# A top-k attention and gated MLP kernel with its slot pipeline made one slot shorter and TensorE's work put in a new order

## The chip, the cores and the metric

The kernel runs on one core of a Trainium2 chip. The core has five engines with instruction streams of their own: TensorE (PE, with its weight loads shown as PEld), VectorE (DVE), ScalarE (ACT), GpSimd (POOL) and SyncE (SP), which issues the transfers. Each works through its stream in the order in which the program was written; they wait for each other by semaphores. The metric is the device time of one execution in microseconds; lower is better.

## The reference, cut to what matters

Attention for 8 batches, 8 heads, 576 queries and keys, 64 numbers per head, in which each query keeps its 32 largest scores only; then a feed-forward block on the heads side by side (4608 tokens of 512 numbers, 2048 hidden), all in float32:

```python
scores = scale * np.matmul(q, k.transpose(0, 1, 3, 2))
kth = np.partition(scores, -top_k, axis=-1)[..., -top_k:-top_k + 1]
scores = np.where(scores >= kth, scores, -1000000000.0)
scores = scores - np.max(scores, axis=-1, keepdims=True)
attn = np.exp(scores)
attn = attn / (np.sum(attn, axis=-1, keepdims=True) + 1e-09)
attn_out = np.matmul(attn, v)
x = attn_out.transpose(0, 2, 1, 3).reshape(B * S, H * D)
h = x @ w_in
g = h * (1.0 / (1.0 + np.exp(-1.702 * h)))
return g @ w_out
```

The two weights come in float64, 16 MB in all, and are rounded to float32 on the chip.

## The kernel before, in words

**Slots.** Work on attention is cut into slots. A slot is 128 queries of a pair of heads, so its scores are a tile `sc` of 128 rows and twice 576 columns. A batch has four full query tiles by four pairs of heads, 16 slots, and the last 64 queries of two pairs put together make two more: 18 slots a batch, N = 144 in all. `slots` lists them in order; before, each batch has its full tiles first and its last queries at the end.

**Stages of a slot.** `scores` (L217) multiplies q by k on TensorE, two heads at once on the two halves of the array's rows, and ScalarE copies the result out (L224). `topk` is a chain of 14 VectorE operations on the two heads: eight times the next eight largest (MAX8, L233), and in between removal of those found (MATCH_REPLACE8, L236). `bounds` makes two small columns on GpSimd (L252, L253); `exponentials` on ScalarE raises what lies below the cut out of the way (L261) and takes the exponential with its sum (L263). `divide` takes the reciprocal of the sums on VectorE (L271, L273) and multiplies both halves of `pr` by it on GpSimd (L276). `turn_main` transposes eight blocks of `pr` on TensorE and `turn_ends` a ninth (L285), with copies on ScalarE (L286). `values` multiplies by v (L308), using half of the array's columns for each head, and ScalarE copies the result into `xT` (L320).

**The feed-forward block.** When all four pairs of a query tile are in `xT`, the tile is `ready`. From then on each slot does one group of four of its sixteen blocks: `hidden` (L349, into one PSUM tile `ph`), `tanh` on ScalarE (L366), `gate` on VectorE (L373, (tanh + 1) times ph, into `gT`), and `project` (L387, added up in `po` over four groups), after which `ob` is copied out (L392) and stored. The last queries of two batches fill one tile of 128 rows together. There are 36 tiles and so 144 groups, as many as there are slots.

**The order in a slot.** Everything is written out by hand, slot by slot, in `slot(n)`; no scheduler changes it. On TensorE it stands as: turn_main of slot n-2, hidden, turn_ends of n-2, prepare (transposes of q and k for coming slots, L187 and L193), scores of n+1, values of n-2, project. On ScalarE: exponentials of n-1, copies of the turn, of prepare, tanh, copies of the scores, of the values, then the rounding of weights for slot n+1. On VectorE: topk of n with the two small operations of `divide` for n-1 after the sixth of its 14, then gate.

**Weights.** The 32 pieces of 128 x 512 are loaded as raw words and rounded in the first slots (`round_piece`): three ScalarE operations (L131 to L133), a shift on VectorE (L137) and two operations on GpSimd (L138, L139). Five pieces belong to slot 0, three to each of the next nine. `pieces` alternates groups of `w_in` and `w_out`.

**Buffers that matter.** `ps_t`, two PSUM buffers, is shared by transposes and values; `ph` has one; `raws` has six; `qkt`, the transposed q and k, five of each.

The functions that the diff touches, with the line numbers of the profile:

Of the kernel before, what the change touches and what calls it, by code (L numbers as in the profile page):

```python
# [8 lines left out]
AF = mybir.ActivationFunctionType  # L9
ALU = mybir.AluOpType  # L10
ENG = mybir.EngineType
F32 = mybir.dt.float32
U32 = mybir.dt.uint32
# [3 lines left out]
P = 128  # L17
# [11 lines left out]
def kernel(  # L29
# [41 lines left out]
    FIRST = (TAIL, 0)  # L71
    MAIN = (0, FULL + 2 * TAIL)
    SCALE = 1.0 / float(D) ** 0.5
    assert D == 64 and 2 * TAIL == P and C == NP * P and C == PIECE and B % 2 == 0
    assert TOPK == 32 and NP == 4 and NF == 4 and NG == 4 and CC == 4

    const = ctx.enter_context(tc.tile_pool(name="const", bufs=1))
    pool = lambda name, bufs, **kw: ctx.enter_context(tc.tile_pool(name=name, bufs=bufs, **kw))
    raws = pool("raws", 6)
    loads = pool("loads", 2)  # L80
    vals = pool("vals", 6)
    qkt = pool("qkt", 5)
    scp = pool("scp", 3)
    prp = pool("prp", 2)
    lefts = pool("lefts", 1)
    small = pool("small", 4)
    ptp = pool("ptp", 2)
    xtp = pool("xtp", 3)
    xtt = pool("xtt", 1)
    gtp = pool("gtp", 3)  # L90
    thp = pool("thp", 2)
    osp = pool("osp", 2)
    ps_s = pool("ps_s", 2, space=PSUM)
    ps_t = pool("ps_t", 2, space=PSUM)
    ps_h = pool("ps_h", 1, space=PSUM)
# [5 lines left out]
    wout = const.tile([P, FC, C], F32, name="wout")  # L101


    pieces = []
    for g in range(NG + 1):
        pieces += [(c, g) for c in range(CC) if g < NG] + [(None, f) for f in range((g - 1) * G, g * G) if g]
    raw = {}

    def load_piece(n):
# [8 lines left out]
    def round_piece(n):  # L118

        c, g = pieces[n]
        dst = wout[:, g, :] if c is None else win[:, c, g * PIECE : (g + 1) * PIECE]
        words = raw.pop(n)[:].rearrange("p (n w) -> p n w", w=2)
        low, high = words[:, :, 0], words[:, :, 1].bitcast(F32)  # L130
        nc.scalar.activation(dst, high, AF.Abs, scale=REBASE)  # L131
        nc.scalar.activation(high, high, AF.Sign)  # L132
        nc.scalar.mul(out=low.bitcast(I32), in_=low, mul=2.0**-29)  # L133

        def shift():
            bits, whole = dst.bitcast(U32), dst.bitcast(I32)
            nc.vector.tensor_scalar(bits, bits, 3, None, op0=ALU.logical_shift_left)  # L137
            nc.gpsimd.tensor_tensor(out=whole, in0=whole, in1=low.bitcast(I32), op=ALU.add)  # L138
            nc.gpsimd.tensor_tensor(out=dst, in0=dst, in1=high, op=ALU.mult)  # L139

        return shift


    qT, kT, vv = {}, {}, {}
# [53 lines left out]

    slots = []
    for b in range(B):  # L200
        slots += [(b, t, (hp, hp)) for t in range(NF) for hp in range(NP)]
        slots += [(b, NF, (hp, hp + 1)) for hp in range(0, NP, 2)]
    N = len(slots)
    PER = N // B
    st = [{} for _ in slots]
# [20 lines left out]
    def topk(n):  # L226

        sc = st[n]["sc"]
        top = st[n]["top"] = small.tile([P, 2, TOPK], F32, name="top")
        left = lefts.tile([P, 2, S], F32, name="left")  # L230

        def largest(r, i):
            nc.vector.max(top[:, i, 8 * r : 8 * r + 8], (left if r else sc)[:, i, :])  # L233

        def remove(r, i):
            nc.vector.match_replace(  # L236
                left[:, i, :], top[:, i, 8 * r : 8 * r + 8], (left if r else sc)[:, i, :], LOWEST
            )

        ops = []  # L240
        for r in range(TOPK // 8):
            ops += [lambda r=r, i=i: largest(r, i) for i in range(2)]
            if r < TOPK // 8 - 1:
                ops += [lambda r=r, i=i: remove(r, i) for i in range(2)]
        return ops
# [22 lines left out]
    def divide(n):  # L268
        den, pr = st[n]["den"], st[n]["pr"]
        some = small.tile([P, 2], F32, name="some")  # L270
        nc.vector.tensor_scalar_add(some[:], den[:], 1e-9)  # L271
        rden = small.tile([P, 2], F32, name="rden")
        nc.vector.reciprocal(rden[:], some[:])  # L273
        for i in range(2):
            on = pr[:, i * S : (i + 1) * S]
            nc.gpsimd.tensor_scalar(on, on, rden[:, i : i + 1], None, op0=ALU.mult)  # L276

    def turn(n, first, cols, blocks):
        pr = st[n]["pr"]
# [8 lines left out]
    def turn_main(n):  # L288
        for i in range(2):
            turn(n, i * NF, MAIN[i], NF)  # L290

    def turn_ends(n):

        turn(n, 2 * NF, FULL, 1)
# [39 lines left out]

    ready = []
    hidden_at = {"g": 0}
    to_gate, to_project = [], []
    proj = {}

    def hidden():  # L340
        if not ready:
            return
        xT, rows = ready[0]
        g = hidden_at["g"]
        ph = ps_h.tile([P, G, P], F32, name="ph")
        for i in range(G):
            f = g * G + i
            for c in range(CC):
                nc.tensor.matmul(  # L349
                    ph[:, i, :],  # L350
                    lhsT=win[:, c, f * P : (f + 1) * P],
                    rhs=xT[:, c, :],
                    start=(c == 0),
                    stop=(c == CC - 1),
                )
        to_gate.append((ph, g, rows))
        hidden_at["g"] = (g + 1) % NG
        if g == NG - 1:
            ready.pop(0)

    def tanh():

        if to_gate and len(to_gate[-1]) == 3:
            ph, g, rows = to_gate.pop()
            th = thp.tile([P, G, P], F32, name="th")
            nc.scalar.activation(th[:], ph[:], AF.Tanh, scale=0.851 / RAISE)  # L366
            to_gate.append((ph, g, rows, th))

    def gate():
        if to_gate:  # L370
            ph, g, rows, th = to_gate.pop()
            gT = gtp.tile([P, G, P], F32, name="gT")
            nc.vector.scalar_tensor_tensor(  # L373
                out=gT[:], in0=th[:], scalar=1.0, in1=ph[:], op0=ALU.add, op1=ALU.mult
            )
            to_project.append((gT, g, rows))

    def project():
        if not to_project:
            return  # L380
        gT, g, rows = to_project.pop(0)
        if g == 0:
            proj["po"] = ps_p.tile([P, C], F32, name="po")
        po = proj["po"]
        for i in range(G):
            f = g * G + i
            nc.tensor.matmul(  # L387
                po[:], lhsT=gT[:, i, :], rhs=wout[:, f, :], start=(f == 0), stop=(f == FC - 1)
            )
        if g == NG - 1:  # L390
            ob = osp.tile([P, C], F32, name="ob")
            nc.scalar.mul(out=ob[:], in_=po[:], mul=0.5 / RAISE**2)  # L392
            for on, row in rows:
                nc.sync.dma_start(out[row : row + on.stop - on.start, :], ob[on, :])
# [4 lines left out]
    def at(n, fn, *args):  # L399
        later.setdefault(n, []).append((fn, args))  # L400

    READY = ((-6, -5), (-2, -1), (-1, 0), (0, 1))
    FETCH = ((-12, -11), (-9, -8), (-5, -4), (-1, 0))
    VALUES = (-8, -7, 1, 2)
    by_slot = {}
    for x in range(NPIECE):
        by_slot.setdefault(max(x - 2, 0) // 3, []).append(x)
    for hp in range(NP):  # L410
        for name in "qk":
            at(max(hp - 2, -1), load, name, 0, hp)
# [6 lines left out]
    for b in range(1, B):  # L419
        for hp in range(NP):  # L420
            for i, name in enumerate("qk"):
                at(b * PER + FETCH[hp][i], load, name, b, hp)
                at(b * PER + READY[hp][i], prepare, name, b, hp)
            at(b * PER + VALUES[hp], load_v, b, hp)
    rounding = {}

    def begin_rounding(n):
        rounding[n] = [round_piece(x) for x in by_slot.get(n, [])]

    def slot(n):  # L430
        todo = later.pop(n, [])
        for fn, args in todo:
            if fn is not prepare:
                fn(*args)
        if 0 <= n - 1 < N:
            bounds(n - 1)
            exponentials(n - 1)
        if 0 <= n - 2 < N:
            turn_main(n - 2)
        hidden()  # L440
        if 0 <= n - 2 < N:
            turn_ends(n - 2)
        for fn, args in todo:
            if fn is prepare:
                fn(*args)
        tanh()
        if n + 1 < N:
            scores(n + 1)
        if 0 <= n - 2 < N:
            values(n - 2)  # L450
        project()
        begin_rounding(n + 1)
        chain = topk(n) if 0 <= n < N else []
        more = rounding.pop(n, [])
        for i, op in enumerate(chain):
            op()
            if i == 5 and 0 <= n - 1 < N:
                divide(n - 1)
            if i and more:
                more.pop(0)()  # L460
        if n == N:
            divide(n - 1)
        gate()

    with tc.manual_schedule():
        for n in range(-1, N + 2):
            slot(n)
        n = N + 2
        while ready or to_project:
            slot(n)  # L470
            n += 1

# [29 lines left out]
```

## Time and profile before

| | |
|---|---|
| time, median of 3 runs | 1684.97 us (1683.83 to 1685.44) |
| span of the profiled run | 1684.1 us |
| TensorE busy | 1596.2 us, 95% |
| VectorE busy | 1539.8 us, 91% |
| ScalarE busy | 1007.0 us, 60% |
| GpSimd busy | 633.7 us, 38% |

A page gives for each engine the time in which it was doing an instruction. Matmuls are pipelined: a new one starts before the last one's end, and their ends are modelled, so for TensorE it is the distance between starts that tells how fast it works. Groups of instructions are named by line, engine, operation and tiles, with their count, busy time, mean length and what ended the idle time before them. VectorE's two groups of the chain, MAX8 and MATCH_REPLACE8, take about 750 ns for each operation; the product on GpSimd (L276) takes 1723 ns, the gate (L373) 677 ns, the copy of a turn (L286) about 470 ns.

### The profile page before, as it was taken

To read this page: it belongs to the slowest core of one execution; us is meant where nothing else is said; L and a number is where in the kernel's file an instruction comes from. 1 tells how busy PE (TensorE), PEld (TensorE's weight loads), DVE (VectorE), ACT (ScalarE), POOL (GpSimd) and SP (SyncE) were. 2 spreads that over 40 slices of the span, in tenths; PEclk is the share of its full clock that TensorE was granted. 3 is DMA by queue.
4 is the path that set the end of the run, shared out by engine and by line. 5 is a ranking of instruction groups with operands and counts; after the bars stand their busy time and mean duration, and the time that the engine had idled before them with its cause. 6 is when DMAs were issued, how large, how long until landed. Compare 5 with 4: busy or idle time off the path is not lost.

```text
span 1684.1 us, 31437 instructions
## 1 busy us (share of the span) xinstructions
PE 1596.2 (95%) x11824; PEld 1176.2 (70%) x11824; DVE 1539.8 (91%) x3344; ACT 1007.0 (60%) x2181; POOL 633.7 (38%) x652
## 2 busy tenths in 40 slices
PE   3459999899999999999999999999999999999998
PEld 2346777677777777777777777777777777777776
DVE  5899999999999999999999999999999999899940
ACT  6787566555655666555655566556665566555530
POOL 5887333333333332333333333333323333333320
PEclk6579999899999999999999999999999999999999
DMA  8341100100101101010000101011010100000000
GB/s 241 119 127 34 28 22 21 42 17 20 36 21 29 29 17 29 13 34 22 21 22 21 36 21 36 15 35 27 16 29 21 35 22 21 22 7 7 7 8 13
DMA packets 125719, 56.55 MB, mean 34 GB/s; under 512 B 116864, under 2 KB 116864, under 8 KB 125568
## 3 DMA queue, kind: packets, MB, share of 16 engines
q1 hardware_dynamic: 125568, 54.55, 12.2%
q8 instruction: 93, 1.52, 0.4%
q14 instruction: 58, 0.48, 0.1%
HBM read 45.09 MB, written 9.44 MB: 32 GB/s over the span
## 4 chain that ended last, share of the span: by engine, by line
PE 90%; ACT 5%; DVE 2%; issue 1%; SPq 1%; POOL 0%; DMA 0%; POOLq 0%; DVEq 0%; ACTq 0%
PE po L387 30%; PE ph L349 30%; PE o L308 11%; PE s_ps L217 10%; PE tp L285 8%; PE tp L187 2%; ACT raw L132 1%; DVE top L233 1%; DVE left L236 1%; ACT raw L133 1%; ACT pr L263 1%; ACT win L131 1%; ACT k_t L189 1%; ACT wout L131 0%; ACT sc L261 0%
## 5 line engine op out<-in xcount | busy, mean ns | idle before, releaser
L276 POOL TENSOR_SCALAR pr<-pr,rden 128x576 f32<-128x576 f32 x288 | 492.9, 1723 | 682.6 <-DVE rden L273 424.7
L233 DVE MAX8 top<-left 128x8 f32<-128x576 f32 x864 | 611.8, 752 | 0.0
L387 PE MATMUL po<-wout,gT 128*128 128x512 f32 x1152 | 532.0, 605 | 0.0
L349 PE MATMUL ph<-xT,win 128*128 128x128 f32 x4096 | 480.0, 276 | 1.9 <-DVE gT L373 1.9
L349 PEld LDWEIGHTS ph<-xT,win 128*128 128x128 f32 x4096 | 469.2, 192 | 3.1 <-DVE gT L373 2.1
L236 DVE MATCH_REPLACE8 left<-top,left 128x576 f32<-128x576 f32 x576 | 423.9, 745 | 0.0
L387 PEld LDWEIGHTS po<-wout,gT 128*128 128x128 f32 x1152 | 207.1, 189 | 229.0 <-issue 227.7
L261 ACT ACTIVATE sc<-sc,cut 128x576 f32<-128x576 f32 x288 | 207.2, 767 | 193.6 <-POOL cut L252 193.6
L286 ACT COPY pt<-tp 128x512 f32<-128x512 f32 (+1 forms) x432 | 188.6, 470 | 219.2 <-PE tp L285 218.8
L285 PEld LDWEIGHTS tp<-ident,pr 128*128 128x128 f32 x1296 | 156.3, 142 | 126.3 <-issue 62.3
L285 PE MATMUL tp<-ident,pr 128*128 128x128 f32 x1296 | 193.3, 276 | 48.2 <-ACT pt L286 44.8
L263 ACT ACTIVATE pr<-sc,low 128x576 f32<-128x576 f32 x288 | 218.9, 761 | 0.0
L233 DVE MAX8 top<-sc 128x8 f32<-128x576 f32 x288 | 204.5, 755 | 12.2 <-ACT sc L224 11.3
L236 DVE MATCH_REPLACE8 left<-top,sc 128x576 f32<-128x576 f32 x288 | 212.9, 751 | 0.0
L224 ACT COPY sc<-s_ps 128x576 f32<-128x576 f32 x288 | 170.4, 645 | 57.3 <-PE s_ps L217 55.2
L217 PE MATMUL s_ps<-k_t,q_t 64*128 64x288 f32 (+1 forms) x1280 | 189.5, 444 | 0.9 <-ACT k_t L189 0.9
L308 PEld LDWEIGHTS o<-pt,v_l 128*64 128x64 f32 x2560 | 131.8, 140 | 58.2 <-ACT th L366 35.5
L308 PE MATMUL o<-pt,v_l 128*64 128x128 f32 (+1 forms) x2560 | 166.0, 274 | 0.0
L373 DVE SCALAR_TENSOR_TENSOR gT<-th,ph 128x512 f32<-128x512 f32 x144 | 97.5, 677 | 54.1 <-ACT th L366 53.8
L252 POOL TENSOR_SCALAR cut<-top 128x2 f32<-128x2 f32 x144 | 31.9, 222 | 273.9 <-DVE top L233 272.8
L217 PEld LDWEIGHTS s_ps<-k_t,q_t 64*128 64x128 f32 (+1 forms) x1280 | 103.1, 183 | 41.4 <-issue 20.5
L366 ACT ACTIVATE th<-ph 128x512 f32<-128x512 f32 x144 | 87.1, 605 | 35.6 <-PE ph L349 35.6
(41 smaller groups left out, 805.0 us busy)
## 6 DMA issues: line engine op xcount, KB each, us to landing
q_l<-in_q_dram SPq DMA_DIRECT2D x64, 128.0 KB, 2.6
k_l<-in_k_dram SPq DMA_DIRECT2D x64, 128.0 KB, 2.5
v_l<-in_v_dram SPq DMA_DIRECT2D x64, 128.0 KB, 2.5
raw<-in_moe_w_in_dram SPq DMA_DIRECT2D x16, 512.0 KB, 4.9
raw<-in_moe_w_out_dram SPq DMA_DIRECT2D x16, 512.0 KB, 3.8
out_dram<-ob SPq DMA_DIRECT2D x32, 256.0 KB, 2.1
ends<-in_q_dram SPq DMA_DIRECT2D x32, 32.0 KB, 2.3
ends<-in_k_dram SPq DMA_DIRECT2D x32, 32.0 KB, 2.4
```

The source lines that it names most:

```text
L217: nc.tensor.matmul(ps[i][rows, c, 0:HALF], lhsT=qT[b, hps[p]][on, cols], rhs=kT[b, hps[p]][on, FIRST[i] + c * HALF : FIRST[i] + (c + 1) * ...
L224: nc.scalar.copy(out=sc[:, i, :].rearrange("p (c k) -> p c k", c=2), in_=ps[i][:, :, 0:HALF])
L233: nc.vector.max(top[:, i, 8 * r : 8 * r + 8], (left if r else sc)[:, i, :])
L236: nc.vector.match_replace(left[:, i, :], top[:, i, 8 * r : 8 * r + 8], (left if r else sc)[:, i, :], LOWEST)
L261: nc.scalar.activation(sc[:, i, :], sc[:, i, :], AF.Prelu, bias=cut[:, i : i + 1], alpha=HUGE)
L263: nc.scalar.activation(pr[:, i * S : (i + 1) * S], sc[:, i, :], AF.Exp, bias=low[:, i : i + 1], accum_out=den[:, i : i + 1],)
L276: nc.gpsimd.tensor_scalar(on, on, rden[:, i : i + 1], None, op0=ALU.mult)
L285: nc.tensor.transpose(tp[:, c * P : (c + 1) * P], pr[:, cols + c * P : cols + (c + 1) * P], ident[:])
L286: nc.scalar.copy(out=to, in_=tp[:, 0 : blocks * P])
L308: nc.tensor.matmul(o[j * D : (j + 1) * D, 0 : cols.stop - cols.start], lhsT=main[:, c, j, :] if c < NF else tail[:, j, :], rhs=pt[:, j * N ...
L349: nc.tensor.matmul(ph[:, i, :], lhsT=win[:, c, f * P : (f + 1) * P], rhs=xT[:, c, :], start=(c == 0), stop=(c == CC - 1),)
L387: nc.tensor.matmul(po[:], lhsT=gT[:, i, :], rhs=wout[:, f, :], start=(f == 0), stop=(f == FC - 1))
```

## The change

It does six things.

1. Each slot n turns and multiplies by the values of slot n-1, not n-2; so the pipeline is a slot shorter, and the division must come before the turn of the same slot.
2. TensorE's order in a slot becomes: prepare, scores of n+1, three of four projection blocks, turn_main, the fourth block, turn_ends, values, hidden. The projection works on a `gT` that is two slots old, so that it has nothing to wait for.
3. The ends of an even batch stand last and those of the odd batch after it first, so that the two are neighbours and their common tile is ready at once.
4. From slot 12 on the gate is moved from VectorE to GpSimd (an addition and a product), and ScalarE copies `ph` to SBUF for it. From slot 11 on ScalarE takes the second half of the division.
5. The steps of weight rounding are spread over the slot in which they are made, in amounts of 3, 3, 3, 3, 4, 4, 4, 4, 4 for slots 0 to 8; their GpSimd part is finished in the next slots. All of `w_in` comes first.
6. Tables of when q, k and v are loaded and prepared, and numbers of buffers, are changed to suit.

The core of it:

```diff
-        slots += [(b, t, (hp, hp)) for t in range(NF) for hp in range(NP)]
-        slots += [(b, NF, (hp, hp + 1)) for hp in range(0, NP, 2)]
+        full = [(b, t, (hp, hp)) for t in range(NF) for hp in range(NP)]
+        ends = [(b, NF, (hp, hp + 1)) for hp in range(0, NP, 2)]
+        slots += ends + full if b % 2 else full + ends
...
-            on = pr[:, i * S : (i + 1) * S]
-            nc.gpsimd.tensor_scalar(on, on, rden[:, i : i + 1], None, op0=ALU.mult)
+            on, by = pr[:, i * S : (i + 1) * S], rden[:, i : i + 1]
+            if i and n >= SETTLED:
+                nc.scalar.activation(on, on, AF.Copy, scale=by)
+            else:
+                nc.gpsimd.tensor_scalar(on, on, by, None, op0=ALU.mult)
...
+            if aside:
+                h = raws.tile([P, G, P], F32, name="h", tag="raw")
+                nc.scalar.copy(out=h[:], in_=ph[:])
+                ph = h
...
+        if aside:
+            nc.gpsimd.tensor_scalar(th[:], th[:], 1.0, None, op0=ALU.add)
+            nc.gpsimd.tensor_tensor(out=gT[:], in0=th[:], in1=h[:], op=ALU.mult)
+        else:
             nc.vector.scalar_tensor_tensor(
-                out=gT[:], in0=th[:], scalar=1.0, in1=ph[:], op0=ALU.add, op1=ALU.mult
+                out=gT[:], in0=th[:], scalar=1.0, in1=h[:], op0=ALU.add, op1=ALU.mult
             )
...
-    READY = ((-6, -5), (-2, -1), (-1, 0), (0, 1))
+    READY = (((-8, -7), (-6, -5), (-4, -3), (-2, -1)), ((-6, -5), (-4, -3), (-2, -2), (-1, -1)))
...
+    by_slot = dict(enumerate([3, 3, 3, 3, 4, 4, 4, 4, 4]))
...
     def slot(n):
         todo = later.pop(n, [])
         for fn, args in todo:
             if fn is not prepare:
                 fn(*args)
-        if 0 <= n - 1 < N:
+        aside = SETTLED < n < N
+        before = 0 <= n - 1 < N
+        if before:
             bounds(n - 1)
             exponentials(n - 1)
-        if 0 <= n - 2 < N:
-            turn_main(n - 2)
-        hidden()
-        if 0 <= n - 2 < N:
-            turn_ends(n - 2)
+        tanh(aside)
+        some = [round_piece(x) for x in by_slot.get(n, [])]
+        for piece in some:
+            piece["size"]()
+        shifts = [piece["shift"] for piece in some]
+        for i, op in enumerate(topk(n) if 0 <= n < N else [lambda: None] * 14):
+            op()
+            if i == 2:
+                while unfinished and unfinished[0][0] < n - 1:
+                    unfinished.pop(0)[1]()
+            if i == 5:
+                if before:
+                    divide(n - 1)
+                for _, fn in unfinished[:2]:
+                    fn()
+                del unfinished[:2]
+            if i == 11 and not aside:
+                gate(aside)
+            if i > 6 and shifts:
+                shifts.pop(0)()
+        if aside:
+            gate(aside)
         for fn, args in todo:
             if fn is prepare:
                 fn(*args)
-        tanh()
         if n + 1 < N:
             scores(n + 1)
-        if 0 <= n - 2 < N:
-            values(n - 2)
-        project()
-        begin_rounding(n + 1)
...
+        for piece in some:
+            piece["sign"]()
+        going = len(to_project) > (2 if n < N else 0)
+        if going:
+            project(range(G - 1))
+        if before:
+            turn_main(n - 1)
+        if going:
+            project(range(G - 1, G))
+        if before:
+            turn_ends(n - 1)
+        for piece in some:
+            piece["low"]()
+            unfinished.append((n, piece["finish"]))
+        if before:
+            values(n - 1)
+        hidden()
```

`SETTLED` is 11. `pool` sizes: raws 6 to 8, qkt 5 to 6, xtp 3 to 2, gtp 3 to 4, osp 2 to 1.

More of the change, by code (lines that the diff above doesn't have):

```diff
@@ L73 @@
     SCALE = 1.0 / float(D) ** 0.5
+    SETTLED = 11
     assert D == 64 and 2 * TAIL == P and C == NP * P and C == PIECE and B % 2 == 0
@@ L78 @@
     pool = lambda name, bufs, **kw: ctx.enter_context(tc.tile_pool(name=name, bufs=bufs, **kw))
-    raws = pool("raws", 6)
+    raws = pool("raws", 8)
     loads = pool("loads", 2)
     vals = pool("vals", 6)
-    qkt = pool("qkt", 5)
+    qkt = pool("qkt", 6)
     scp = pool("scp", 3)
@@ L87 @@
     ptp = pool("ptp", 2)
-    xtp = pool("xtp", 3)
+    xtp = pool("xtp", 2)
     xtt = pool("xtt", 1)
-    gtp = pool("gtp", 3)
+    gtp = pool("gtp", 4)
     thp = pool("thp", 2)
-    osp = pool("osp", 2)
+    osp = pool("osp", 1)
     ps_s = pool("ps_s", 2, space=PSUM)
@@ L101 @@
     wout = const.tile([P, FC, C], F32, name="wout")
-    pieces = []
-    for g in range(NG + 1):
-        pieces += [(c, g) for c in range(CC) if g < NG] + [(None, f) for f in range((g - 1) * G, g * G) if g]
+    pieces = [(c, g) for g in range(NG) for c in range(CC)] + [(None, f) for f in range(FC)]
     raw = {}
@@ L130, in round_piece, with finish @@
         low, high = words[:, :, 0], words[:, :, 1].bitcast(F32)
[L131 to L137, printed above, removed]
+        bits, whole = dst.bitcast(U32), dst.bitcast(I32)
+        def finish():
             nc.gpsimd.tensor_tensor(out=whole, in0=whole, in1=low.bitcast(I32), op=ALU.add)
             nc.gpsimd.tensor_tensor(out=dst, in0=dst, in1=high, op=ALU.mult)
-        return shift
+        return {
+            "size": lambda: nc.scalar.activation(dst, high, AF.Abs, scale=REBASE),
+            "shift": lambda: nc.vector.tensor_scalar(bits, bits, 3, None, op0=ALU.logical_shift_left),
+            "sign": lambda: nc.scalar.activation(high, high, AF.Sign),
+            "low": lambda: nc.scalar.mul(out=low.bitcast(I32), in_=low, mul=2.0**-29),
+            "finish": finish,
+        }
     qT, kT, vv = {}, {}, {}
@@ L336 @@
     hidden_at = {"g": 0}
-    to_gate, to_project = [], []
+    to_gate, gated, to_project = [], [], []
     proj = {}
@@ L359, in hidden, with tanh @@
             ready.pop(0)
-    def tanh():
-        if to_gate and len(to_gate[-1]) == 3:
+    def tanh(aside):
+        if to_gate:
             ph, g, rows = to_gate.pop()
@@ L366, in tanh, with gate, project @@
             nc.scalar.activation(th[:], ph[:], AF.Tanh, scale=0.851 / RAISE)
[L367 to L372, printed above, removed]
+            if aside:
+                h = raws.tile([P, G, P], F32, name="h", tag="raw")
+                nc.scalar.copy(out=h[:], in_=ph[:])
+                ph = h
+            gated.append((th, ph, g, rows))
+    def gate(aside):
+        if not gated:
+            return
+        th, h, g, rows = gated.pop()
+        gT = gtp.tile([P, G, P], F32, name="gT")
+        if aside:
+            nc.gpsimd.tensor_scalar(th[:], th[:], 1.0, None, op0=ALU.add)
+            nc.gpsimd.tensor_tensor(out=gT[:], in0=th[:], in1=h[:], op=ALU.mult)
+        else:
             nc.vector.scalar_tensor_tensor(
-                out=gT[:], in0=th[:], scalar=1.0, in1=ph[:], op0=ALU.add, op1=ALU.mult
+                out=gT[:], in0=th[:], scalar=1.0, in1=h[:], op0=ALU.add, op1=ALU.mult
             )
[L376 to L383, printed above, removed]
+        to_project.append((gT, g, rows))
+    def project(blocks):
+        if blocks[0] == 0:
+            proj["on"] = to_project.pop(0)
+            if proj["on"][1] == 0:
+                proj["po"] = ps_p.tile([P, C], F32, name="po")
+        gT, g, rows = proj["on"]
         po = proj["po"]
-        for i in range(G):
+        for i in blocks:
             f = g * G + i
@@ L389, in project @@
             )
-        if g == NG - 1:
+        if blocks[-1] == G - 1 and g == NG - 1:
             ob = osp.tile([P, C], F32, name="ob")
@@ L400, in at @@
         later.setdefault(n, []).append((fn, args))
-    READY = ((-6, -5), (-2, -1), (-1, 0), (0, 1))
[L405 to L409, printed above, removed]
+    READY = (((-8, -7), (-6, -5), (-4, -3), (-2, -1)), ((-6, -5), (-4, -3), (-2, -2), (-1, -1)))
+    FETCH = (((-12, -11), (-10, -9), (-6, -5), (-4, -3)), ((-10, -9), (-8, -7), (-5, -4), (-3, -2)))
+    VALUES = ((-8, -7, -1, 0), (-8, -7, 0, 0))
+    by_slot = dict(enumerate([3, 3, 3, 3, 4, 4, 4, 4, 4]))
+    for n in by_slot:
+        first = sum(map(len, list(by_slot.values())[:n]))
+        by_slot[n] = list(range(first, first + by_slot[n]))
+    assert by_slot[len(by_slot) - 1][-1] == NPIECE - 1
     for hp in range(NP):
@@ L421 @@
             for i, name in enumerate("qk"):
[L422 to L428, printed above, removed]
+                at(b * PER + FETCH[b % 2][hp][i], load, name, b, hp)
+                at(b * PER + READY[b % 2][hp][i], prepare, name, b, hp)
+            at(b * PER + VALUES[b % 2][hp], load_v, b, hp)
+    unfinished = []
     def slot(n):
@@ L445, in slot @@
                 fn(*args)
-        tanh()
         if n + 1 < N:
             scores(n + 1)
-        if 0 <= n - 2 < N:
-            values(n - 2)
-        project()
-        begin_rounding(n + 1)
[L453 to L463, printed above, removed]
+        for piece in some:
[15 more added lines that the diff above has]
+        hidden()
     with tc.manual_schedule():
-        for n in range(-1, N + 2):
+        for n in range(-1, N + 1):
             slot(n)
-        n = N + 2
-        while ready or to_project:
+        n = N + 1
+        while ready or to_gate or gated or to_project:
             slot(n)
```

## The prediction

> **What bounds the kernel now.** I read the page's busy shares and slices first, then busy time by stage, then the timeline of TensorE.
>
> ```profile
> PE 1596.2 (95%) x11824; PEld 1176.2 (70%) x11824; DVE 1539.8 (91%) x3344; ACT 1007.0 (60%) x2181; POOL 633.7 (38%) x652
> PE   3459999899999999999999999999999999999998
> PEclk6579999899999999999999999999999999999999
> PE 90%; ACT 5%; DVE 2%; issue 1%; SPq 1%; POOL 0%; DMA 0%; POOLq 0%; DVEq 0%; ACTq 0%
> ```
> ```profile
> 0.00:177.60 177.60, 107.27 (x663) 77.51 (x664) 148.38 (x301) 130.52 (x258) 127.91 (x122) 0.77 0.44 127
> 420.00:1610.00 1190.00, 1184.30 (x8948) 874.67 (x8947) 1146.03 (x2508) 715.92 (x1571) 415.01 (x437) 1.00 0.09 23
> ```
>
> From 420 to 1610 us TensorE is busy 99.5% at full clock and VectorE 96%: TensorE sets the pace, VectorE is just under it. The loss is in the head: up to 177.6 us TensorE has 107 us, part of it at a low clock. Busy TensorE is not TensorE at its peak, so one ordinary slot (starts in us, then modelled lengths, which overlap; read the differences of starts):
>
> ```profile
> 166.93 1.04 PE L285 MATMUL tp<-ident,pr 128*128 128x128 f32 x8
> 167.80 3.74 PE L349 MATMUL ph<-xT,win 128*128 128x128 f32 x32
> 171.37 0.27 PE L285 MATMUL tp<-ident,pr 128*128 128x128 f32 x1
> 171.58 1.24 PE L217 MATMUL s_ps<-k_t,q_t 64*128 64x288 f32 x8
> 172.75 1.09 PE L308 MATMUL o<-pt,v_l 128*64 128x128 f32 x16
> 173.67 0.39 PE L308 MATMUL o<-pt,v_e 128*64 128x128 f32 x4
> 173.99 3.70 PE L387 MATMUL po<-wout,gT 128*128 128x512 f32 x8
> 177.53 1.04 PE L285 MATMUL tp<-ident,pr 128*128 128x128 f32 x8
> ```
> ```profile
> 1637.66 3.60 PE L387 MATMUL po<-wout,gT 128*128 128x512 f32 x8
> 1641.10 3.73 PE L349 MATMUL ph<-xT,win 128*128 128x128 f32 x32
> ```
>
> The slot is 177.53 - 166.93 = 10.60 us. The numbers before the tile sizes matter: `128*128` is the whole array, `64*128` (scores) and `128*64` (values) are halves of it. Where the mode changes, time goes. Eight projection matmuls after the hidden ones, same mode, take 1641.10 - 1637.66 = 3.44; after the values they take 177.53 - 173.99 = 3.54, and the last four values matmuls take 0.32 where 20 at 0.92/16 = 0.058 each would give 0.23: this switch costs 0.10 + 0.09 = 0.19. A transpose takes 0.87/8 = 0.11, but 0.21 ahead of the scores (+0.10), and the first pair of score matmuls starts its successor 0.34 later, not 0.24 as the others do in the trace (+0.10): 0.20. Scores to values, in the same way, 0.09 + 0.05 = 0.14. Sum 0.53; without them the slot would be 10.07.
>
> **What the Trainium skill says.** "TensorEngine Tiling (Array Packing)", Key Properties: changing the tiling mode, not just the tile, drains TensorE. The trace agrees: 0.14 to 0.20 us at each of three changes per slot. "TensorE: Matmul & The Clock Gate", Part 1: idle time throttles the clock, sustained work releases it; the trace has 0.77 as the mean clock to 177.6 us and 1.00 later. "SBUF — State Buffer", two separate sides: VectorE and GpSimd share a port pair, and a GpSimd operation can block certain VectorE forms. I see none of it here: MAX8 is 755 ns whether GpSimd is busy or not.
>
> **The change, part by part.**
>
> *Gate and one division moved* (slots 12 on, about 132 of each). VectorE loses 132 x 0.68 = 89 us of busy time and its slot falls from 10.50 (first MAX8 at 808.75, the next slot's at 819.25) to about 9.9 us. It was not the bound, so this hides. GpSimd loses a 1.72 us division and gains an add (estimate 1.72 x 512/576 = 1.53) and a product (1.33, the L139 row): 5.0 of a 10.8 us slot with the rest. ScalarE gains a copy of ph (about 0.5, as L286) and a multiplication (0.76): about 7.7 us of the slot. Both fit. What is queued behind the gate on GpSimd is `bounds`, and exponentials, division and transposes wait for that; but the gate can start 1.3 us after the hidden matmuls end and is done 2.9 us later, while `top` is ready about 5.4 us after that end (see next: the small operations end 0.1 us before it, and eight of VectorE's fourteen, 5.5 us, follow). No loss.
>
> *Pipeline a slot shorter.* Turning slot n-1 now waits for a division of the same slot. In the steady state exponentials start when the values copy ends, 3.3 us before the next slot begins on TensorE, and take 2.9; then 0.3 for VectorE's two small operations, 1.72 on GpSimd, done 1.7 us into the slot. TensorE reaches the turn after scores (1.2) and three projections (2.7), at 3.9. The wait is hidden with 2 us to spare; that is what the three projections ahead of it do.
>
> *The new order* is the cost that I find. Per slot it is hidden, scores, projection, turn, projection, turn ends, values, hidden. The modes are whole, half, whole, half, whole: four changes where there were three. To scores 0.20, scores to projection about 0.19, to values 0.14 (seen in the tail, where values follow a transpose), values to hidden about 0.19: 0.72 against 0.53, so +0.19 a slot, 10.79. Over 132 slots: +25 us. Interleaving projection and transposes stays in one mode and costs nothing (project to turn: eight at 0.43 leave no gap).
>
> *Weight steps spread.* A piece costs ScalarE 1.82, GpSimd 2.65, VectorE 0.34.
>
> ```profile
> 95.09 1.28 POOL L138 TENSOR_TENSOR wout<-wout,raw 128x512 int32<-128x512 int32 x1
> 96.45 1.28 POOL L139 TENSOR_TENSOR wout<-wout,raw 128x512 f32<-128x512 f32 x1
> 97.72 3.42 POOL L276 TENSOR_SCALAR pr<-pr,rden 128x576 f32<-128x576 f32 x2
> ```
>
> Slot 0 shrinks from 19 us to some 13, since VectorE's chain no longer waits for five pieces. Slots 4 to 8 then carry four pieces: GpSimd 4 x 2.65 + 3.42 + 0.4 = 14.4, ScalarE 4 x 1.82 + 2.9 + 0.5 + 1.2 + 1.4 + 0.3 = 13.6 plus a wait for the hidden matmuls; before, 14 with three pieces. Slots 1 and 2, with ScalarE's prepare copies in line behind the exponentials, about 16.5. Walking the slots so, TensorE begins slot 12 at 186 us (about 183 by hand, plus 3 for raw buffers that free only after the previous slot's leftovers). By then it has eight hidden steps and turns up to slot 10 behind it; before, at 177.6, six and slot 9.
>
> *Last queries side by side.* Hidden steps then run in every slot from 4 to 147, none missing. Before, slots 22 and 23 have none, and batch 1 took 194.7 us (projections from 240.9 to 435.6) where 196.8 - 14 of work would do: 12 us lost. That returns. The tail shortens from eight slots to four with hidden steps, but TensorE was full there, so it is no further gain.
>
> *Prepares.* Where q and k of a pair come in one slot, `ends` waits for q's copy:
>
> ```profile
> 628.06 0.66 PE L187 MATMUL tp<-ident,k_l 128*128 128x128 f32 x4
> 629.40 0.66 PE L187 MATMUL tp<-ident,q_l 128*128 128x128 f32 x4 [0.58 <-ACT k_t L189]
> ```
>
> About 0.75 us, two slots in each of seven batches: 10.5. After, two slots in four odd batches, but the copy stands behind tanh, copy and multiplication on ScalarE, about 1.6: 13. Even.
>
> **The sum.** Slot 12 at 186; 132 slots x 10.79 = 1424; prepares 31 (each q +0.40, each k +0.72, 28 of each), their waits 13, ends slots 1; slot 143 has no scores, -1; the tail's slots 9.5 + 3 x 7.0 + 3 x 3.44 = 41; last copy and store 4.7 as before; device time over span 0.9. About 1700; I say 1699. The same sum for before, from 177.6, gives 1687 (measured 1685).
>
> **Rivals.** (1) *The fourth mode change is free* (weights loaded ahead, or the new pairs cheaper): -25, 1674. Against it: all three kinds seen cost 0.14 or more. (2) *Half of that, or a head some 13 us better*: 1686, no change. GpSimd's 32 pieces plus divisions sum to about 125 us from 23 us on, so slot 12 can hardly begin before 174. (3) *The shorter pipeline binds*: GpSimd's gate slower than priced, or ScalarE's line late, so the turn waits. My 2 us of slack must be used up; 0.3 us a slot on top gives 1739. For it: ScalarE is strictly in order and gets most of the added work.
>
> **How the numbers follow.** Forecast 0.60, (1) 0.18, (2) 0.12, (3) 0.10. Faster 0.20, same 0.10, slower 0.70. The range takes in the head (174 to 195 for slot 12), the switch (0.10 to 0.30) and most of (1): 1674 to 1716.
>
> **What would show it.** Right: projection starts 10.8 apart in ordinary slots, gaps of 0.2 at scores to projection and values to hidden; VectorE near 1450 us busy, GpSimd near 790, ScalarE near 1180; no idle TensorE ahead of the turn after slot 12; the first hidden matmuls at 85 to 92 us. Wrong: slots of 10.6, TensorE waiting on pr, or slot 12 before 175.

## The result and the profile after

The changed kernel takes 1693.13 us (1693.03 to 1693.74) where the kernel before takes 1685.2: the ratio is 1.0048, with a 95% interval of 1.0031 to 1.0066. It is slower by 8 us, though VectorE, the second busiest engine, has less to do. First the page after: busy times, two rows of its slices and the chain by engine.

```profile
PE 1619.8 (96%) x11824; PEld 1174.1 (69%) x11824; DVE 1464.1 (87%) x3212; ACT 1154.8 (68%) x2446; POOL 771.5 (46%) x783
PE   4678999999999999999999999999999999999999
PEclk7679999999999999999999999999999999999999
PE 88%; ACT 6%; POOL 3%; DVE 1%; issue 1%; DMA 1%; SPq 1%; POOLq 0%; ACTq 0%
```

VectorE lost 76 us of busy time, ScalarE gained 148 and GpSimd 138, and TensorE, with the same 11824 matmuls, is busy 24 us longer. Busy time by stage (columns: stage, its length, then busy time of TensorE, its weight loads, VectorE, ScalarE and GpSimd, the granted clock, and transfers):

```profile
0.00:177.60 177.60, 121.55 (x731) 88.45 (x732) 145.74 (x305) 129.13 (x262) 129.08 (x122) 0.79 0.45 127
420.00:1610.00 1190.00, 1180.94 (x8778) 856.87 (x8777) 1069.26 (x2359) 824.18 (x1752) 521.21 (x537) 1.00 0.09 23
```

In the head (to 177.6 us) TensorE does 731 matmuls where it did 663, so the head is better. From 420 us to 1610 us it does 8778 where it did 8948, with the clock full and the engine busy 99.2%. The loss is in this stage, in which TensorE is never seen waiting for long. The timeline of TensorE in one ordinary slot shows where:

```profile
685.71 1.24 PE L221 MATMUL s_ps<-k_t,q_t 64*128 64x288 f32 x8
686.88 2.84 PE L404 MATMUL po<-wout,gT 128*128 128x512 f32 x6
689.56 1.04 PE L292 MATMUL tp<-ident,pr 128*128 128x128 f32 x8
690.44 1.02 PE L404 MATMUL po<-wout,gT 128*128 128x512 f32 x2
691.30 0.27 PE L292 MATMUL tp<-ident,pr 128*128 128x128 f32 x1
691.50 1.09 PE L315 MATMUL o<-pt,v_l 128*64 128x128 f32 x16
692.42 0.39 PE L315 MATMUL o<-pt,v_e 128*64 128x128 f32 x4
692.74 3.84 PE L356 MATMUL ph<-xT_t,win 128*128 128x128 f32 x32
696.51 1.24 PE L221 MATMUL s_ps<-k_t,q_t 64*128 64x288 f32 x8
```

The slot is 696.51 - 685.71 = 10.80 us; it was 10.60. Read downwards which part of the array each row uses (`64*128`, `128*128`, `128*64`): this mode changes at 686.88, 691.50, 692.74 and 696.51, four times. Six projection matmuls take 2.68 us after the scores, where six at 0.43 are 2.57; the hidden ones take 3.77 from their start to the scores', where they took 3.57 in the kernel before with no change on either side; the two projection matmuls after the turn take 0.86, just two at 0.43, since that step stays in one mode.

The wait for q's copy, in a slot that prepares q and k of one pair, is the only wait of TensorE's matmuls that the list of waits has from 200 us to 1620 (columns: in total, times, longest):

```profile
PE tp L195 <- ACT q_t L191: 11.6, 8, 1.5
```

The list counts from the modelled end of the matmul before. By the distance of starts each of the eight costs 1.6 us (1.72, where 0.11 would do without a wait), 12.9 in all. The kernel before has 14 shorter waits in its prepares, 9.5 us in all by the distance of starts.

### The profile page after: what moved, and what is told of

Read it like the earlier page. It is cut to its first block, busy times and chain, and to the rows that moved or that the text cites. A ratio compares the mean times of both kernels' runs of the same rounds, so it can differ in the third digit from the quotient of the medians.

```text
span 1691.4 us, 31717 instructions
## 1 busy us (share of the span) xinstructions
PE 1619.8 (96%) x11824; PEld 1174.1 (69%) x11824; DVE 1464.1 (87%) x3212; ACT 1154.8 (68%) x2446; POOL 771.5 (46%) x783
## 4 chain that ended last, share of the span: by engine, by line
PE 88%; ACT 6%; POOL 3%; DVE 1%; issue 1%; DMA 1%; SPq 1%; POOLq 0%; ACTq 0%
PE po L404 30%; PE ph L356 29%; PE o L315 10%; PE s_ps L221 10%; PE tp L292 8%; ACT pr L267 1%; POOL pr L283 1%; PE tp L189 1%; ACT raw L140 1%; ACT sc L265 1%; ACT raw L141 1%; POOL wout L134 0%; DVE left L240 0%; DMA raw<-in_moe_w_out_dram 0%; POOL win L134 0%
## 5 line engine op out<-in xcount | busy, mean ns | idle before, releaser
L283 POOL TENSOR_SCALAR pr<-pr,rden 128x576 f32<-128x576 f32 x155 | 268.4, 1733 | 723.0 <-PE ph L356 621.9
L404 PE MATMUL po<-wout,gT 128*128 128x512 f32 x1152 | 555.4, 606 | 0.0
L356 PE MATMUL ph<-xT,win 128*128 128x128 f32 x4096 | 495.3, 280 | 0.0
L293 ACT COPY pt<-tp 128x512 f32<-128x512 f32 (+1 forms) x432 | 192.6, 481 | 247.8 <-PE tp L292 247.6
L404 PEld LDWEIGHTS po<-wout,gT 128*128 128x128 f32 x1152 | 196.7, 190 | 194.8 <-issue 194.6
L237 DVE MAX8 top<-sc 128x8 f32<-128x576 f32 x288 | 201.9, 743 | 11.5 <-ACT sc L228 11.5
L386 POOL TENSOR_SCALAR th<-th 128x512 f32<-128x512 f32 x132 | 197.3, 1495 | 0.0
L221 PE MATMUL s_ps<-k_t,q_t 64*128 64x288 f32 (+1 forms) x1280 | 185.2, 436 | 0.5 <-ACT k_t L191 0.5
L275 DVE TENSOR_SCALAR some<-den 128x2 f32<-128x2 f32 x144 | 28.1, 195 | 168.2 <-ACT pr L267 168.2
L387 POOL TENSOR_TENSOR gT<-th,h 128x512 f32<-128x512 f32 x132 | 168.6, 1277 | 11.0
```

Source lines behind the costliest of these rows:

```text
L221: nc.tensor.matmul(ps[i][rows, c, 0:HALF], lhsT=qT[b, hps[p]][on, cols], rhs=kT[b, hps[p]][on, FIRST[i] + c * HALF : FIRST[i] + (c + 1) * ...
L283: nc.gpsimd.tensor_scalar(on, on, by, None, op0=ALU.mult)
L293: nc.scalar.copy(out=to, in_=tp[:, 0 : blocks * P])
L356: nc.tensor.matmul(ph[:, i, :], lhsT=win[:, c, f * P : (f + 1) * P], rhs=xT[:, c, :], start=(c == 0), stop=(c == CC - 1),)
L386: nc.gpsimd.tensor_scalar(th[:], th[:], 1.0, None, op0=ALU.add)
L404: nc.tensor.matmul(po[:], lhsT=gT[:, i, :], rhs=wout[:, f, :], start=(f == 0), stop=(f == FC - 1))
```

## Experiments

Two theories stand against each other. **Mode changes**: TensorE sets the pace in both kernels, and a fourth change of its array mode per slot costs 0.2 us. **Moved work**: the gate, the copy of `ph` and the division on their new engines, or waits in the shorter pipeline, lengthen the slot.

**Three mode changes in the changed kernel.** Scores go between the turn's end and values, so that the two half-array stages are neighbours from slot 12 on; all moved work stays moved.

```diff
-        if n + 1 < N:
+        late = SETTLED < n
+        if n + 1 < N and not late:
             scores(n + 1)
...
             unfinished.append((n, piece["finish"]))
+        if n + 1 < N and late:
+            scores(n + 1)
         if before:
             values(n - 1)
```

> The changed kernel with one edit: from slot 12 on the scores stand between turn_ends and values, so the two half-array stages are neighbours and the mode changes three times a slot, not four. Theory (the fourth change costs 0.19 us a slot): ordinary slots of 10.60 us between projection starts, 132 x 0.19 = 25 us less than the changed kernel, about 1668, faster than before by 1%. Rival (the gate's and the division's new places or waits in the shorter pipeline lengthen the slot): about 1693, unchanged, or longer, since scores come later and VectorE waits for them.

Measured: 1665.78 us, ratio to before 0.9878 (0.9862 to 0.9895), 27 us under the changed kernel. Its TensorE timeline around the neighbours:

```profile
810.58 1.24 PE L221 MATMUL s_ps<-k_t,q_t 64*128 64x288 f32 x8
811.75 1.10 PE L315 MATMUL o<-pt,v_l 128*64 128x128 f32 x16
812.68 0.39 PE L315 MATMUL o<-pt,v_e 128*64 128x128 f32 x4
813.00 3.84 PE L356 MATMUL ph<-xT,win 128*128 128x128 f32 x32
816.67 0.60 PE L189 MATMUL tp<-ident,q_l 128*128 128x128 f32 x4
817.11 2.74 PE L404 MATMUL po<-wout,gT 128*128 128x512 f32 x6
819.69 1.04 PE L292 MATMUL tp<-ident,pr 128*128 128x128 f32 x8
...
821.62 1.24 PE L221 MATMUL s_ps<-k_t,q_t 64*128 64x288 f32 x8
```

From scores to scores it is 11.04, less 0.44 for the four transposes of q: 10.60. Six projections now take 819.69 - 817.11 = 2.58, without the 0.1 of a change. The slot is as short as in the kernel before, so moved work and the shorter pipeline don't lengthen an ordinary slot.

**Four mode changes in the kernel before.**

```diff
         if n + 1 < N:
             scores(n + 1)
+        project()
         if 0 <= n - 2 < N:
             values(n - 2)
-        project()
```

> The kernel before with one edit: project stands between scores and values, so the mode changes four times a slot. Nothing else moves. Theory: slots of 10.79 us, about 137 x 0.19 = 26 us more than before, 1711. Rival (the slot of 10.8 in the changed kernel comes from the moved gate, the copy of ph and the shorter pipeline): no change, 1685.

Measured: 1726.41 us, ratio 1.0241 (1.0225 to 1.0256). The direction is the theory's, but 40 us is too much. The fourth projection starts at 171.7 us, 8.3 later than before, so part of the loss is in the head; probably values wait there behind a projection, which was not traced further. So the edit was made again from slot 12 on only.

```diff
+        if n >= 12:
+            project()
         if 0 <= n - 2 < N:
             values(n - 2)
-        project()
+        if n < 12:
+            project()
```

> The kernel before with project between scores and values from slot 12 on only, so that the head stays as it was. Theory: the head's own loss in the earlier run (its fourth projection starts 8 us later than before) goes, and what stays is the longer slot, 0.24 us by 127 slots or so: 1685 + 30 = 1715. Rival (the loss is not in the mode changes but in the order's waits): less than 10 us over before.

Measured: 1716.41 us, ratio 1.0171 (1.0156 to 1.0187). TensorE there:

```profile
808.22 1.24 PE L217 MATMUL s_ps<-k_t,q_t 64*128 64x288 f32 x8
809.39 3.70 PE L387 MATMUL po<-wout,gT 128*128 128x512 f32 x8
813.02 1.09 PE L308 MATMUL o<-pt,v_l 128*64 128x128 f32 x16
813.95 0.39 PE L308 MATMUL o<-pt,v_e 128*64 128x128 f32 x4
814.26 1.15 PE L285 MATMUL tp<-ident,pr 128*128 128x128 f32 x8
815.25 3.74 PE L349 MATMUL ph<-xT,win 128*128 128x128 f32 x32
818.83 0.27 PE L285 MATMUL tp<-ident,pr 128*128 128x128 f32 x1
819.03 1.20 PE L217 MATMUL s_ps<-k_t,q_t 64*64 64x288 f32 x16
```

819.03 - 808.22 = 10.81 (the median from projection to projection is 10.84), with no gate moved and no pipeline shortened. Four changes cost what they cost in the changed kernel, in a kernel that shares the number of changes with it, but neither the order nor the moved work. Eight projections take 3.63, not 3.54, and eight transposes after values 0.99, not 0.87.

**Gate and division back.**

```diff
-    SETTLED = 11
+    SETTLED = 1000
```

> The changed kernel with SETTLED at 1000, so that the gate stays on VectorE and both halves of the division on GpSimd; order and pipeline as changed. Theory (TensorE bounds at 10.79 a slot; VectorE needs 10.5): same as the changed kernel within 5 us, 1690 to 1698. Rival (the moved gate loads ScalarE and GpSimd and costs time): faster by 10 us or more. Second rival (VectorE is near enough to the bound that moving the gate saved much): slower by 15 us or more.

Measured: 1685.15 us, ratio 0.9993 (0.9984 to 1.0002): 8 us under the changed kernel and the same as the kernel before. That is outside the theory's range and just short of the first rival's. The ordinary slot is the same in both, 10.80, so the engine moves cost and bring nothing there:

```profile
681.05 1.24 PE L221 MATMUL s_ps<-k_t,q_t 64*128 64x288 f32 x8
691.85 1.24 PE L221 MATMUL s_ps<-k_t,q_t 64*128 64x288 f32 x8
```

The 8 us are elsewhere, and the waits of TensorE name the place:

```profile
PE tp L195 <- ACT q_t L191: 2.4, 8, 0.3
```

It was 11.6. On ScalarE the copy of q no longer stands behind the copy of `ph` and the division, and 9.2 of the 11.6 us go. So without its engine moves the whole change neither costs nor gains; with them it costs 8 us.

**One prepare a slot.** The tables of even batches, which prepare q and k in different slots, serve all batches; other buffers make room for it:

```diff
-    qkt = pool("qkt", 6)
+    qkt = pool("qkt", 7)
...
-    gtp = pool("gtp", 4)
-    thp = pool("thp", 2)
+    gtp = pool("gtp", 3)
+    thp = pool("thp", 1)
...
-                at(b * PER + FETCH[b % 2][hp][i], load, name, b, hp)
-                at(b * PER + READY[b % 2][hp][i], prepare, name, b, hp)
+                at(b * PER + FETCH[0][hp][i], load, name, b, hp)
+                at(b * PER + READY[0][hp][i], prepare, name, b, hp)
```

> The changed kernel with q and k of all batches prepared one tile a slot (the even batches' tables for all; qkt 7, and gtp 3 and thp 1 to make room). Theory: the eight waits of TensorE for the copy of q, 1.45 us each in the trace, go: -12 us, 1681. Rival (TensorE catches up elsewhere, since other slots wait anyway): less than 3 us.

Measured: 1678.37 us, ratio 0.9963 (0.995 to 0.9976): 15 us under the changed kernel, and TensorE's list of waits from 200 us to 1600 is empty. The waits were lost time, 12.9 us by the distance of starts; the expectation had 12 from the list. The numbers of buffers changed along with the tables and were not tested apart.

**Last queries at each batch's end.**

```diff
-        slots += ends + full if b % 2 else full + ends
+        slots += full + ends
...
-                at(b * PER + FETCH[b % 2][hp][i], load, name, b, hp)
-                at(b * PER + READY[b % 2][hp][i], prepare, name, b, hp)
-            at(b * PER + VALUES[b % 2][hp], load_v, b, hp)
+                at(b * PER + FETCH[1][hp][i], load, name, b, hp)
+                at(b * PER + READY[1][hp][i], prepare, name, b, hp)
+            at(b * PER + VALUES[1][hp], load_v, b, hp)
```

> The changed kernel with the last queries of every batch at its end, as before; the tables of loads and prepares are those of odd batches for all. Theory: two slots near 200 us lose their hidden and projection groups and wait for VectorE, about +12 us, and six more slots have q and k in one slot at about 1.5 us of waiting each, +9: about 1714. Rival (the side by side order brings nothing because TensorE is full in the tail): +9 from the prepares alone, 1702.

Measured: 1725.36 us, ratio 1.0234 (1.0219 to 1.025): 32 us over the changed kernel, 11 more than expected. TensorE's waits:

```profile
PE tp L195 <- ACT q_t L191: 20.3, 14, 1.5
PE tp L292 <- POOL pr L283: 17.0, 8, 4.4
```

Waits for q's copy rose from 11.6 to 20.3, the 9 expected. Unexpected were eight waits for `pr`: two next to the slots without a group, 4.4 us each, and six of 1.4 in later batches. One of the six, ScalarE and then TensorE:

```profile
560.21 0.27 ACT L327 COPY xT<-o 128x128 f32<-128x128 f32 x1 [4.75 <-PE ph L356]
560.37 1.44 ACT L265 ACTIVATE sc<-sc,cut 128x576 f32<-128x576 f32 x2
```
```profile
565.71 0.55 PE L292 MATMUL tp<-ident,pr 128*128 128x128 f32 x3 [1.59 <-POOL pr L283]
```

A copy into `xT` waits 4.75 us for hidden matmuls, and the exponentials, and with them the division, stand behind it on ScalarE. The reading is that in this order groups run later than their tile, so that an older `xT` still has readers and two buffers are too few. With three:

```diff
-    xtp = pool("xtp", 2)
+    xtp = pool("xtp", 3)
...
-    gtp = pool("gtp", 4)
+    gtp = pool("gtp", 3)
```

> The run with the last queries at each batch's end, with three xT buffers instead of two (gtp 3 to make room). In the earlier run TensorE waited six times, 8.2 us in all, for pr after a copy into xT had waited for the hidden matmuls of an older tile. Theory (the order makes the second buffer short): those six waits go, 1717. Rival (they come from the division on GpSimd): unchanged, 1725.

Measured: 1716.14 us, ratio 1.0176 (1.0161 to 1.0192). Those six waits are gone, the other two stay (8.8 us). So the order is worth 23 us against this run, 9 of them in prepares; about 14 is what the missing groups cost. There VectorE sets the pace (stretch, its length, then busy time of TensorE, its weight loads, VectorE, ScalarE and GpSimd, the granted clock, and transfers):

```profile
285.00:295.00 10.00, 5.35 (x38) 3.82 (x39) 9.97 (x24) 6.35 (x13) 2.11 (x3) 0.71 0.00 0
```

Beside that, with the last queries side by side two `xT` buffers are enough.

**Three changes and single prepares together.**

> Both edits together: three mode changes from slot 12 on and one prepare a slot. Theory: both gains add, -25 and -12 from 1693: 1656, 1.7% faster than before. Rival (a next bound is near, as VectorE waits for later scores): gains under 25 in sum.

Measured: 1651.84 us, ratio 0.9805 (0.9788 to 0.9821), 41 us under the changed kernel: 27 and 15 add up. The list of waits has none of TensorE's matmuls from 200 us to 1600. It is the fastest kernel here, 2% under the kernel before. But the division now ends only 0.3 us ahead of the turn (median), where it was 2.0 in the changed kernel. Since the engine moves had brought nothing to the ordinary slot, they were taken back in it:

```diff
-    SETTLED = 11
+    SETTLED, LATE = 1000, 11
...
-        late = SETTLED < n
+        late = LATE < n
```

> Three mode changes and single prepares, with the gate back on VectorE and both halves of the division on GpSimd. Theory (TensorE bounds at 10.62 a slot, VectorE needs 10.5): 1652 as with the gate moved, within 4 us. Rival (with TensorE's slot cut to 10.62, VectorE's 10.5 binds together with its waits): slower by 8 us or more.

Measured: 1771.6 us, ratio 1.0504 (1.0487 to 1.0522). The theory falls. The rival's number came (slower by more than 8 us), but not its reason: VectorE's load is not the bound, as it waits 1.1 us a slot itself. The slot is 11.71 us. GpSimd, TensorE and VectorE:

```profile
801.15 3.42 POOL L283 TENSOR_SCALAR pr<-pr,rden 128x576 f32<-128x576 f32 x2 [5.29 <-DVE rden L277]
```
```profile
804.63 0.66 PE L292 MATMUL tp<-ident,pr 128*128 128x128 f32 x4 [0.34 <-POOL pr L283]
...
806.19 1.24 PE L221 MATMUL s_ps<-k_t,q_t 64*128 64x288 f32 x8
```
```profile
808.20 1.42 DVE L237 MAX8 top<-sc 128x8 f32<-128x576 f32 x2 [1.10 <-ACT sc L228]
...
812.50 0.17 DVE L277 RECIPROCAL rden<-some 128x2 f32<-128x2 f32 x1
```

It is a ring of waits. Scores start at 806.19 and VectorE's chain on them at 808.20; the reciprocal for the slot before stands behind the chain's first six operations and ends at 812.67. GpSimd's two products, shown for the slot before at 801.15, come 11.71 later at 812.86 and end at 816.3, and only then can the turn end that stands ahead of the next scores. Once around the ring is the slot, whatever each engine's load. In the run with scores ahead of the turn the same two products on GpSimd left the slot at 10.80, so scores behind the turn belong to the ring. A division on two engines at once takes half of the products' 3.42 off it, which would bring it to 10.0 by estimate, under 10.6. To tell division from gate, only the gate went back:

```diff
-        aside = SETTLED < n < N
+        aside = False
```

> Three mode changes and single prepares, with the gate on VectorE but the division's second half on ScalarE. In the run with both moved back a ring of waits set the slot: scores 2.0 us to VectorE's start, 4.5 to the reciprocal, 3.6 for two products on GpSimd, 1.6 for turn, projection and ends to the next scores, 11.7 in sum. Theory (the division alone closed that ring): it falls to 10.0, TensorE bounds again at 10.62, 1652 within 5 us. Rival (VectorE's 10.5 with the gate was the cause): 1700 or more.

Measured: 1652.66 us, ratio 0.9802 (0.9784 to 0.9819). So splitting the division is enough to open the ring, and the gate can stay on VectorE at no cost.

## Why the prediction came out

It was right in direction and within 6 us of the time, though the rise itself, forecast as 14 us, was 8. Most of its terms can be checked one by one.

- *TensorE sets the pace, and the new order adds a mode change.* Slot 10.79 predicted, 10.80 measured. Both directions were shown: a change taken out gives 27 us back, one put into the kernel before costs 30 (against its 1686.49 in the same comparison).
- *Moved work hides.* Shown for the ordinary slot. ScalarE is busy 1155 us (1180 forecast), GpSimd 772 (790), VectorE 1464 (1450): on VectorE the gate had taken only 0.59 us from its start to the next operation's, not the 0.68 of its length, which the forecast of 1450 takes off. It does not hide in the eight slots with two prepares, where it costs 8 us, so "no loss" holds for the ordinary slot alone. Under prepares the prediction had these waits right (about 1.6 us each, behind the copy and the multiplication on ScalarE, as in the trace), but it called their sum of 13 "even" with the kernel before, where it reckoned 10.5 and the trace has 9.5.
- *The shorter pipeline has 2 us to spare.* Shown: the division ends 2.0 us before the turn starts (median of the ordinary slots), and there is no wait of TensorE for `pr` from 180 us on.
- *Last queries side by side bring 12 us.* About 14 by the experiment. The clock, read as 1.00 after the head, falls once more there: in the kernel before it is 0.64 from 300 to 305 us. VectorE is busy 4.97 of these 5 us, so no loss by the slower clock itself is shown.
- *The head.* This is the term that was mis-sized. Slot 12 was put at 186 us; its first matmul is at 180.3. The first hidden matmul, expected from 85 to 92 us, is at 78.3. VectorE's first MAX8 of slots 0 to 3:

```profile
10.70 1.42 DVE L237 MAX8 top<-sc 128x8 f32<-128x576 f32 x2 [10.70 <-ACT sc L228]
22.23 1.42 DVE L237 MAX8 top<-sc 128x8 f32<-128x576 f32 x2 [0.78 <-ACT sc L228]
36.16 1.39 DVE L237 MAX8 top<-sc 128x8 f32<-128x576 f32 x2
49.91 1.40 DVE L237 MAX8 top<-sc 128x8 f32<-128x576 f32 x2
```

Slots 0 to 2 take 11.5, 13.9 and 13.8 us, where 13, 16.5 and 16.5 were forecast. That is 7 us, of which 5.7 are left at slot 12. Which part of the 16.5 was too long can't be said, since the prediction doesn't break it up. Nor does its floor of 174 us for slot 12 follow from what it gives: 125 us from 23 us on end at 148. From slot 12 on the sum holds: it has 1468 us for the 132 slots with their prepares and waits, and the trace has 1466.6 (180.33 to 1646.97).

Against the kernel before, the head is better. At the same place that kernel stands at 177.5 us, with two hidden groups, one turn and one multiplication by v less behind it. So the 8 us come out as a balance: about +26 from the mode changes, +3 from the waits in prepares (12.9 against 9.5), -12 to -14 from the missing groups, and -6 from the head (2.8 later, with 9.3 us of TensorE work more done). That makes 9 to 11, so 1 to 3 us stay unassigned. The rival of a free mode change and the rival of a pipeline that binds did not come about in the changed kernel, though the latter did in the run with both moves taken back and scores behind the turn.

## What to carry to other kernels

Where TensorE sets the pace and is busy all the time, count the changes of its array mode as work. Here stages that use half the array were best side by side, and each change that an order added lengthened the slot by about 0.2 us, though TensorE was never seen waiting. Moving work off an engine that doesn't set the pace brought nothing by itself, and in slots where another engine's copy stood behind the moved work it cost time. But it can shorten a ring of waits, and then an order that was too slow becomes the fast one. Add up the ring (who waits for whom, once around) before moving a stage, not only each engine's load.

## What the runs showed of the hardware

On GpSimd the addition of a constant, with one input tile, takes longer than the product of two tiles of the same size: 1495 ns against 1277 for 128 x 512 in float32. The prediction had 1530 and 1330 from rows of the kernel before, so the order could be seen there already.

A mode change into transposes costs about as much as one into matmuls: eight transposes take 0.99 us after values and 0.87 after a projection, and eight projection matmuls take 3.54 after values and 3.44 in one mode.
